# Tile 3's norm ahead of tile 4's statistics on VectorE, and its epsilon added there

## The chip, the cores and the metric

The kernel runs on one core of one Trainium2 chip. The metric is device time of one execution in microseconds (us), and the numbers quoted are medians of executions.

## The reference

```python
xn = _layernorm(x)                 # x: 2048 tokens x 1024, bf16
s  = attention(xn, wqkv, wo)       # 32 heads of 32
g  = silu(mlp(layernorm(xn)))      # 1024 -> 3584 -> 1024
return x + s * g
```

Only the first layer norm matters here. It is done by tiles of 128 tokens, 16 in all, in the first 35 us.

## The kernel before

All instructions are recorded first, in one order for each engine, with semaphores from the data dependences. These parts touch the change (cuts are marked):

```python
def bn_half(tb, c):   # statistics of half a tile, VectorE
    op("vector", lambda e: e.bn_stats(stats[:, tb, c, :], ...), ...)      # L324
def bn_merge(tb):
    op("vector", lambda e: e.bn_aggr(mv[:, tb, :], ...), ...)             # L328
def stat(tb):
    bn_half(tb, 0); bn_half(tb, 1); bn_merge(tb)

def rstd(lo, hi):     # 1/sqrt(var + eps)
    op("vector" if hi == 1 else "gpsimd", ... e.tensor_scalar(L(0), mv[:, lo:hi, 1], EPS, ...))   # L338
    op("gpsimd", ... e.tensor_tensor(L(2), L(0), mhalf[...], op=ALU.pow))                          # L340

def xnorm(tb):        # (x - mean) * rstd, 128x1024 bf16, VectorE
    op("vector", ... e.tensor_scalar(xnb[i], xst[...], mv[:, tb, 0:1], lnp[:, 2, tb:tb + 1], ...)) # L359

def transp(tb):       # tiles 0 to 5: TensorE (L386), copied out by ScalarE
    if tb >= TDMA:    # TDMA = 6: the others by a DMA transpose (L379)
        op("sync", lambda e: e.dma_start_transpose(xnT[:, :, tb * 128:(tb + 1) * 128], xnb[i]), ...)
    ...

def norm_pair(p):
    lo, hi = 2 * p, 2 * p + 2
    if p == 0:
        stat(0); rstd(0, 1); stat_scalar(1); xnorm(0); xnorm(1)
        stat(2); rstd(2, 3); stat(3); xnorm(2); rstd(3, 4)
    elif p == 1:
        stat(4); xnorm(3); stat(5); rstd(4, 6)
    else:
        if p < NP - 1: stat(hi)
        for t in (lo, lo + 1):
            xnorm(t)
            if t >= TDMA: transp(t)
        if p + 1 < NP: stat(hi + 1); rstd(hi, hi + 2)
    ...
```

(Several calls are put on one line here.) Each pair of tiles then gets its K and Q projections (L687), the transposes of a later pair (L386), its V projection (L703) and one step of attention (L867, L879, L896, L899).

The softmax here doesn't subtract the row's maximum and nothing guards it: scores larger than these inputs give would overflow.

Of the kernel before, what the change touches and what calls it, by code (L numbers as in the profile page):

```python
# [7 lines left out]
ALU = mybir.AluOpType  # L8
# [27 lines left out]
class _Prog:  # L36
# [52 lines left out]
    def op(self, eng, fn, r=(), w=(), dma=None, after=(), c=200.0):  # L89
        deps = list(after)  # L90
        rdy = self.ready(eng, r, w, after)
        same_raw = eng in ("vector", "scalar", "gpsimd")
        for k in r:
            o = self.lastw.get(k)
            if o is not None and (dma or o.dsem or o.eng != eng or same_raw):
                deps.append(o)
        for k in w:
            o = self.lastw.get(k)
            if o is not None and (dma or o.dsem or o.eng != eng or same_raw):
                deps.append(o)  # L100
            for o in self.readers[k].values():
                if dma or o.dsem or o.eng != eng or same_raw:
                    deps.append(o)
        dcount = None
        if dma:
            prev = self.dlast.get(dma)
            if prev is not None:
                deps.append(prev)
            dcount = 16 + (prev.dcount if prev is not None else 0)
        x = _Op(eng, len(self.lists[eng]), fn, deps, dma, dcount)  # L110
        if dma and self.dlast.get(dma) is not None:
            rdy = max(rdy, self.dlast[dma].t)
        self.clock(x, eng, dma, c, rdy)
        if dma:
            self.dlast[dma] = x
        self.lists[eng].append(x)
        self.order.append(x)
        for k in r:
            self.n += 1
            self.readers[k][(eng, self.n) if dma else eng] = x  # L120
        for k in w:
            self.lastw[k] = x
            self.readers[k] = {}
        return x
# [44 lines left out]
def bass_recurrent_scan__mha_block__mixer_channel_mlp__prompt_kernel(  # L169
# [28 lines left out]
    EPS = 1e-5  # L198
# [9 lines left out]
    with ExitStack() as st:  # L208
        pg = _Prog(nc, st)
        op = pg.op  # L210

        def sb(name, shape, dt):
            return st.enter_context(nc.sbuf_tensor(name, list(shape), dt))
# [30 lines left out]
        mv = sb("mv", [128, NT, 2], F32)  # L244
# [78 lines left out]
        def bn_half(tb, c):  # L323
            op("vector", lambda e: e.bn_stats(stats[:, tb, c, :], xst[:, tb * D + c * 512:tb * D + (c + 1) * 512]),  # L324
               r=[("xst", tb)], w=[("st", tb, c)], c=677.0)

        def bn_merge(tb):
            op("vector", lambda e: e.bn_aggr(mv[:, tb, :], stats[:, tb, :, :].rearrange("p c s -> p (c s)")),  # L328
               r=[("st", tb, 0), ("st", tb, 1)], w=[("mv", tb)], c=209.0)

        def stat(tb):
            bn_half(tb, 0)
            bn_half(tb, 1)
            bn_merge(tb)

        def rstd(lo, hi):
            L = lambda k: lnp[:, k, lo:hi]
            op("vector" if hi == 1 else "gpsimd", lambda e: e.tensor_scalar(L(0), mv[:, lo:hi, 1], EPS, None, op0=ALU.add),  # L338
               r=[("mv", t) for t in range(lo, hi)], w=[("l0", t) for t in range(lo, hi)], c=169.0)
            op("gpsimd", lambda e: e.tensor_tensor(L(2), L(0), mhalf[:, 0:hi - lo], op=ALU.pow), r=[("l0", t) for t in range(lo, hi)] + ["mhalf"],  # L340
               w=[("l2", t) for t in range(lo, hi)], c=708.0)

        def ycoef(b):
            lo, hi = 2 * b, 2 * b + 2
            L = lambda k: lnp[:, k, lo:hi]
            l2k = [("l2", t) for t in range(lo, hi)]
            mvk = [("mv", t) for t in range(lo, hi)] + [("var", 1)] * (b == 0)
            op("gpsimd", lambda e: e.tensor_tensor(L(4), mv[:, lo:hi, 1], L(2), op=ALU.mult), r=mvk + l2k, w=[("l4", b)])
            op("gpsimd", lambda e: e.tensor_tensor(L(4), L(4), L(2), op=ALU.mult), r=[("l4", b)] + l2k, w=[("l4", b)])
            op("gpsimd", lambda e: e.tensor_scalar(L(4), L(4), EPS, None, op0=ALU.add), r=[("l4", b)], w=[("l4", b)])  # L350
            op("gpsimd", lambda e: e.tensor_tensor(L(5), L(4), mhalf[:, 0:2], op=ALU.pow), r=[("l4", b), "mhalf"], w=[("l5", b)], c=760.0)
            op("gpsimd", lambda e: e.tensor_tensor(L(6), L(2), L(5), op=ALU.mult), r=[("l5", b)] + l2k, w=[("l6", b)])
            if b < 2:
                op("gpsimd", lambda e: e.tensor_tensor(L(7), mv[:, lo:hi, 0], L(6), op=ALU.mult), r=[("l6", b)] + mvk, w=[("l7", b)])
                op("gpsimd", lambda e: e.tensor_scalar(L(7), L(7), -1.0, None, op0=ALU.mult), r=[("l7", b)], w=[("l7", b)])

        def xnorm(tb):
            i = tb % NXN
            op("vector", lambda e: e.tensor_scalar(xnb[i], xst[:, tb * D:(tb + 1) * D], mv[:, tb, 0:1], lnp[:, 2, tb:tb + 1],  # L359
                                                   op0=ALU.subtract, op1=ALU.mult), r=[("xst", tb), ("mv", tb), ("l2", tb)], w=[("xnb", i)], c=545.0)  # L360
# [15 lines left out]
        def transp(tb):  # L376
            i = tb % NXN
            if tb >= TDMA:
                op("sync", lambda e: e.dma_start_transpose(xnT[:, :, tb * 128:(tb + 1) * 128], xnb[i]),  # L379
                   r=[("xnb", i)], w=[("xnT", tb)], dma=f"xt{tb % 4}", c=380)  # L380
                return
            bk = pro_bank()

            def f(e):
                for dc in range(DC):
                    ins = e.transpose(bankb(bk)[:, dc * 128:(dc + 1) * 128], xnb[i][:, dc * 128:(dc + 1) * 128], ident[:])  # L386
                return ins
            op("tensor", f, r=[("xnb", i), "ident"], w=[("b", bk)], c=("full", 8, 128))
            op("scalar", lambda e: e.activation(xnT[:, :, tb * 128:(tb + 1) * 128],
                                                bankb(bk)[:, 0:D].rearrange("p (c t) -> p c t", c=DC), ACT.Copy),  # L390
               r=[("b", bk)], w=[("xnT", tb)], c=903.0)
# [318 lines left out]
        def stat_scalar(tb):  # L710
            xt = xst[:, tb * D:(tb + 1) * D]
            mean, neg, sq = mv[:, tb, 0:1], mneg[:, 0:1], mneg[:, 1:2]
            op("scalar", lambda e: e.activation(xnb[8], xt, ACT.Identity, scale=-1.0 / D, accum_out=neg), r=[("xst", tb)], w=[("xnb", 8), "mneg"], c=903.0)
            op("scalar", lambda e: e.activation(xnb[8], xt, ACT.Square, bias=neg, accum_out=sq), r=[("xst", tb), "mneg"], w=[("xnb", 8), "msq"], c=903.0)  # L714
            op("scalar", lambda e: e.activation(mean, neg, ACT.Copy, scale=-1.0), r=["mneg"], w=[("mv", tb)], c=50.0)
            op("gpsimd", lambda e: e.tensor_scalar(lnp[:, 0, tb:tb + 1], sq, 1.0 / D, EPS, op0=ALU.mult, op1=ALU.add), r=["msq"], w=[("l0", tb)])
            op("gpsimd", lambda e: e.tensor_tensor(lnp[:, 2, tb:tb + 1], lnp[:, 0, tb:tb + 1], mhalf[:, 0:1], op=ALU.pow), r=[("l0", tb), "mhalf"],
               w=[("l2", tb)], c=708.0)
            op("gpsimd", lambda e: e.tensor_scalar(mv[:, tb, 1:2], sq, 1.0 / D, None, op0=ALU.mult), r=["msq"], w=[("var", tb)])
# [4 lines that stand above are left out]
                stat(0)  # L724
                rstd(0, 1)
                stat_scalar(1)
                xnorm(0)
                xnorm(1)
                stat(2)
                rstd(2, 3)  # L730
                stat(3)
                xnorm(2)
                rstd(3, 4)
            elif p == 1:
                stat(4)
                xnorm(3)
                stat(5)
                rstd(4, 6)
            else:
                if p < NP - 1:  # L740
                    stat(hi)
                for t in (lo, lo + 1):
                    xnorm(t)
                    if t >= TDMA:
                        transp(t)
                if p + 1 < NP:
                    stat(hi + 1)
                    rstd(hi, hi + 2)
            if p < 2:
                ycoef(p)  # L750
# [8 lines left out]
        for p in range(3):  # L759
            norm_pair(p)  # L760
# [186 lines left out]
        while u < NU + LAG or state["qi"] < total or dq or act_tasks or due:  # L947
# [13 lines left out]
            if u >= NP - 1 and state["qi"] < total:  # L961
# [8 lines left out]
                if entry:  # L970
                    it, lo, hi = entry
# [82 lines left out]
```

## Time and profile before

| | before |
|---|---|
| median of 3 runs at the outset | 1090.87 us (1089.76 to 1091.55) |
| span of the profiled run | 1087.7 us |
| TensorE, ScalarE, VectorE, GpSimd busy | 99%, 96%, 58%, 2% |
| transpose of tile 3 begins on TensorE | 13.29 us |
| chain on TensorE and ScalarE alone | from 13.3 us to nearly the end |

The prediction shows the views. One more line is needed, of the timeline of TensorE's weight loads (start, length, engine, line, what, idle time before it and what ended it; no bracket means no idle time):

```profile
13.29 0.45 PEld L386 LDWEIGHTS ps<-ident,hT 128*128 128x128 bf16 x8 [1.16 <-DVE hT L359]
...
17.58 0.99 PEld L386 LDWEIGHTS ps<-ident,hT 128*128 128x128 bf16 x16
```

Tile 3's transpose comes after 1.16 us of idle time, ended by VectorE's norm. The transposes of tiles 4 and 5 follow at 17.58 without a wait.

### The profile page before, as it was taken

To read this page: it belongs to the slowest core of one execution; us is meant where nothing else is said; L and a number is where in the kernel's file an instruction comes from. 1 tells how busy PE (TensorE), PEld (TensorE's weight loads), DVE (VectorE), ACT (ScalarE), POOL (GpSimd) and SP (SyncE) were. 2 spreads that over 40 slices of the span, in tenths; PEclk is the share of its full clock that TensorE was granted. 3 is DMA by queue.
4 is the path that set the end of the run, shared out by engine and by line. 5 is a ranking of instruction groups with operands and counts; after the bars stand their busy time and mean duration, and the time that the engine had idled before them with its cause. 6 is when DMAs were issued, how large, how long until landed. Compare 5 with 4: busy or idle time off the path is not lost.

```text
span 1087.7 us, 61820 instructions
## 1 busy us (share of the span) xinstructions
PE 1077.0 (99%) x29156; PEld 700.9 (64%) x29156; DVE 627.3 (58%) x1395; ACT 1043.5 (96%) x1197; POOL 22.6 (2%) x70
## 2 busy tenths in 40 slices
PE   8999999999999999999999999999999999999998
PEld 5766666666666666666666666666666666666665
DVE  7388843477732576642377743378733377635556
ACT  7899998999999999999999999999999999999993
POOL 4400000000000000000000000000000000000000
PEclk9999999999999999999999999999999999999999
DMA  8844365423364224345333264423254333675434
GB/s 247 169 139 137 111 172 149 121 61 110 109 164 122 65 63 120 109 104 148 90 100 100 69 161 119 125 81 109 81 132 119 91 119 108 198 201 107 108 92 124
DMA packets 209336, 131.92 MB, mean 121 GB/s; under 512 B 52538, under 2 KB 200250, under 8 KB 209082
## 3 DMA queue, kind: packets, MB, share of 16 engines
q1 hardware_dynamic: 209082, 127.97, 42.8%
q8 instruction: 228, 3.74, 1.4%
q14 instruction: 26, 0.21, 0.1%
HBM read 104.87 MB, written 12.06 MB: 107 GB/s over the span
## 4 chain that ended last, share of the span: by engine, by line
PE 54%; ACT 44%; DVE 1%; DMA 0%; issue 0%; POOL 0%; SPq 0%
ACT P L879 40%; PE ps L395 32%; PE ps L867 9%; PE ps L896 5%; PE ps L899 5%; ACT u L565 4%; PE ps L703 1%; PE ps L687 1%; ACT thz L609 0%; DVE stats L324 0%; DMA OT<-in_A_x_dram 0%; DVE wq L669 0%; PE ps L386 0%; DVE hT L359 0%; ACT hT L714 0%
## 5 line engine op out<-in xcount | busy, mean ns | idle before, releaser
L879 ACT ACTIVATE P<-ps 128x1024 bf16<-128x1024 f32 x1024 | 968.7, 1085 | 8.6 <-PE ps L867 4.0
L896 PE MATMUL ps<-P,VP 128*32 128x256 bf16 x4096 | 256.3, 273 | 0.0
L899 PE MATMUL ps<-P,ones 128*32 128x256 bf16 x4096 | 256.2, 273 | 0.0
L395 PE MATMUL ps<-yTc,war 128*32 128x352 bf16 (+1 forms) x5376 | 225.3, 309 | 0.0
L395 PE MATMUL ps<-hT,war 128*32 128x352 bf16 (+1 forms) x5376 | 225.2, 309 | 0.0
L867 PE MATMUL ps<-QT,KT 32*128 32x256 bf16 x4096 | 203.4, 273 | 2.9 <-ACT P L879 0.2
L395 PEld LDWEIGHTS ps<-hT,war 128*32 128x32 bf16 x5376 | 127.9, 96 | 73.9 <-issue 25.1
L395 PEld LDWEIGHTS ps<-yTc,war 128*32 128x32 bf16 x5376 | 127.4, 96 | 74.2 <-DVE xb L548 19.0
L867 PEld LDWEIGHTS ps<-QT,KT 32*128 32x128 bf16 x4096 | 60.7, 92 | 114.9 <-issue 60.0
L605 DVE TENSOR_SCALAR zh<-ps,b2h 128x352 f32<-128x352 f32 (+1 forms) x48 | 27.5, 572 | 182.3 <-PE ps L395 182.3
L571 DVE SCALAR_TENSOR_TENSOR hT<-u,xb 128x352 bf16<-128x352 f32 (+1 forms) x168 | 84.4, 510 | 68.4 <-ACT u L565 68.4
L548 DVE TENSOR_SCALAR xb<-ps,b1T 128x352 f32<-128x352 f32 (+1 forms) x168 | 96.3, 573 | 47.7 <-PE ps L395 42.8
L896 PEld LDWEIGHTS ps<-P,VP 128*32 128x32 bf16 x4096 | 109.1, 97 | 20.4 <-issue 1.3
L899 PEld LDWEIGHTS ps<-P,ones 128*32 128x32 bf16 x4096 | 109.2, 97 | 18.7
L395 PE MATMUL ps<-xnT,wq 128*32 128x352 bf16 (+1 forms) x2688 | 112.7, 309 | 0.0
L395 PEld LDWEIGHTS ps<-xnT,wq 128*32 128x32 bf16 x2688 | 63.7, 96 | 37.2 <-DVE xb L548 9.1
L558 DVE SCALAR_TENSOR_TENSOR u<-u,xb 128x352 f32<-128x352 f32 (+1 forms) x168 | 82.6, 510 | 1.9
L554 DVE TENSOR_TENSOR u<-xb 128x352 f32<-128x352 f32 (+1 forms) x168 | 82.6, 508 | 0.7
L565 ACT ACTIVATE u<-u 128x704 f32<-128x704 f32 (+1 forms) x84 | 71.9, 861 | 0.0
L395 PE MATMUL ps<-xnT,OT 128*32 128x352 bf16 (+2 forms) x1568 | 62.9, 306 | 0.2 <-DVE wq L669 0.2
L395 PE MATMUL ps<-wq,xnT 128*32 128x256 bf16 x1536 | 50.8, 274 | 0.0
L395 PEld LDWEIGHTS ps<-xnT,OT 128*32 128x32 bf16 x1568 | 37.7, 96 | 19.9 <-DVE wq L669 7.7
(61 smaller groups left out, 477.6 us busy)
## 6 DMA issues: line engine op xcount, KB each, us to landing
war<-in_B_w_dram SPq DMA_DIRECT2D x336, 256.0 KB, 3.3
wq<-in_A_wqkv_dram SPq DMA_DIRECT2D x36, 128.0 KB, 2.4
OT<-in_A_x_dram SPq DMA_DIRECT2D x16, 256.0 KB, 5.5
xnT<-in_A_x_dram SPq DMA_DIRECT2D x16, 256.0 KB, 3.2
out_dram<-wq SPq DMA_DIRECT2D x15, 256.0 KB, 2.0
y_scratch<-OT SPq DMA_DIRECT2D x14, 256.0 KB, 2.6
gT_scratch<-gst SPq DMA_DIRECT2D x32, 88.0 KB, 3.1
xnT<-in_A_wo_dram SPq DMA_DIRECT2D x8, 256.0 KB, 3.9
```

The costliest lines, as they stand in the source:

```text
L395: ins = e.matmul(outs(j), lhsT=lhs(j), rhs=rhs, start=start, stop=stop, tile_position=(0, 32 * j), skip_group_check=True)
L548: x0 = op("vector", lambda e: e.tensor_scalar(xb[:, 0:n], bank(bk, 0, n), b1T[:, f:f + 1], None, op0=ALU.add), r=[("b", bk), "b1"], w=[kx] ...
L554: x = op("vector", lambda e: e.tensor_tensor(ub[:, 0:n], xb[:, 0:n], xb[:, 0:n], op=ALU.mult), r=[kx], w=[ku], c=151 + 1.042 * n)
L558: x = op("vector", lambda e: e.scalar_tensor_tensor(ub[:, 0:n], ub[:, 0:n], 1.0 / 0.044715, xb[:, 0:n], op0=ALU.add, op1=ALU.mult), r=[kx, ...
L565: x = op("scalar", lambda e: e.activation(ut[:, :, 0:n], ut[:, :, 0:n], ACT.Tanh, scale=0.7978845608028654 * 0.044715), r=kus, w=kus, c=48 ...
L571: op("vector", lambda e: e.scalar_tensor_tensor(hT[:, fq, 0:n], ut[:, i, 0:n], 1.0, xq[:, 0:n], op0=ALU.add, op1=ALU.mult), r=[kus[i], kq] ...
L605: x0 = op("vector", lambda e: e.tensor_scalar(zh[:, 0:n], bank(bk, 0, n), 0.25, b2h[:, nb:nb + 1], op0=ALU.mult, op1=ALU.add), r=[("b", bk ...
L687: ins = e.matmul(bank(bk, off, off + 256), lhsT=wq[:, which, dc, 0:128], rhs=xnT[:, dc, t0:t0 + 256], start=dc == 0, stop=dc == DC - 1, sk ...
L867: ins = e.matmul(bank(bks[j], kh * 256, (kh + 1) * 256), lhsT=KT[i2][32 * j:32 * j + 32, k0:k0 + 128], rhs=QT[i2][32 * j:32 * j + 32, qb * ...
L879: op("scalar", lambda e, p=p, sl=sl: e.activation(pb[:, 2 * p:2 * p + 2, :, :].rearrange("p a b q -> p (a b q)"), ps[:, sl * 1024:(sl + 1) ...
L896: e.matmul(bankq(ACC, j, 0, QW), lhsT=VP[vp][:, kb, vo + 32 * j:vo + 32 * j + 32], rhs=pb[:, j, kh, :], start=first, stop=False, tile_posi ...
L899: ins = e.matmul(bankq(ACC, j, QW, 2 * QW), lhsT=ones[:, 0:32], rhs=pb[:, j, kh, :], start=False, stop=last, tile_position=(0, 32 * j), sk ...
```

## The change

TensorE waits for tile 3's norm while VectorE works on the statistics of tile 4. The change turns these two round. So that the norm finds its factor sooner, epsilon is added on VectorE, right after the merge, and GpSimd is left with the power alone.

```diff
-            op("vector" if hi == 1 else "gpsimd", lambda e: e.tensor_scalar(L(0), mv[:, lo:hi, 1], EPS, None, op0=ALU.add),
+            op("vector" if hi in (1, 4) else "gpsimd", lambda e: e.tensor_scalar(L(0), mv[:, lo:hi, 1], EPS, None, op0=ALU.add),
...
                 stat(3)
+                rstd(3, 4)
                 xnorm(2)
-                rstd(3, 4)
+                xnorm(3)
             elif p == 1:
                 stat(4)
-                xnorm(3)
                 stat(5)
                 rstd(4, 6)
```

## The prediction

> **What bounds the kernel now.** I read the page first, then the chain of waits, then the timeline of the first 35 us, which is all that the change touches.
>
> ```profile
> PE 1077.0 (99%) x29156; PEld 700.9 (64%) x29156; DVE 627.3 (58%) x1395; ACT 1043.5 (96%) x1197; POOL 22.6 (2%) x70
> PE 54%; ACT 44%; DVE 1%; DMA 0%; issue 0%; POOL 0%; SPq 0%
> ```
>
> The first line is busy time by engine, the second the share of each engine in the chain that ended last. TensorE and ScalarE bound the kernel in turn; VectorE has 1% of the chain, about 11 of 1087.7 us, and that piece lies in the opening. The chain over the first 16 us shows it:
>
> ```profile
> 7.60 0.55 DVE hT L359
> 8.15 1.21 DVE stats L324 x2
> 9.38 0.21 DVE mv L328
> 9.59 1.16 DVE stats L324 x2
> 10.77 0.21 DVE mv L328
> 10.98 0.41 DVE hT L359
> 11.39 1.21 DVE stats L324 x2
> 12.62 0.21 DVE mv L328
> 12.83 0.42 DVE hT L359
> 13.30 0.62 PE ps L386 x8
> 13.92 1.75 PE ps L703 x16
> ```
>
> Columns: start, length, what. From 7.60 VectorE works without a break: statistics of tiles 2 and 3, norm of tile 2 (10.98), statistics of tile 4 (11.39 to 12.83), norm of tile 3 (12.83 to 13.25). Then TensorE transposes tile 3 (L386) and is in the chain alone until 56.3 us, where ScalarE takes over. So tile 4's statistics, 1.44 us, stand in the chain ahead of the one norm that TensorE waits for. That is what the change attacks. TensorE idles there for 1.16 us by its own row, further down.
>
> GpSimd's timeline tells why the norm was put behind the statistics:
>
> ```profile
> 11.06 0.41 POOL L338 TENSOR_SCALAR lnp<-mv 128x1 f32<-128x1 f32 x1 [0.52 <-DVE mv L328]
> 11.55 0.56 POOL L340 TENSOR_TENSOR lnp<-lnp,mhalf 128x1 f32<-128x1 f32 x1
> 12.95 0.86 POOL L351 TENSOR_TENSOR lnp<-lnp,mhalf 128x2 f32<-128x2 f32 x1
> ```
>
> Tile 3's epsilon add takes 0.41 (0.22 for tile 2 at 9.67) and its power ends at 12.11, well after tile 2's norm is issued; the statistics fill that hole.
>
> **What the Trainium skill says.** (1) "SBUF — State Buffer", section "Who interferes with whom": VectorE's two-port modes, which a tensor_scalar can enter, take a port pair that GpSimd needs, for the whole instruction, and the one that comes second waits. The trace agrees for an operation that starts inside a norm: the add at 11.06 ends at 11.47, 0.08 after the norm of tile 2 ended (11.39); the power at 12.95 ends at 13.81, 0.57 after the norm of tile 3 ended (13.24), and it takes 0.86 against 0.70 for the same one, undisturbed, at 35.49. A norm that starts just after a GpSimd operation is not visibly delayed (34.33: 0.55). (2) "Perfetto Trace Analysis", section "DMA Instruction — HWDGE (DVE, Sync)": the profiled span of a DMA instruction leaves out the data movement. The trace agrees: the transposes' issues take 1.3 us at the median, and their landings 2.7 to 5.4, so landings have to be looked at by themselves. No other page bears on the argument.
>
> **The change, part by part.** *Added on VectorE:* one 128x1 add. Tile 0's twin started 0.24 after its merge (4.98 to 5.22) and took 0.15. Tile 3's merge starts at 10.77, so the add runs 11.01 to 11.16. VectorE starts a next instruction about 0.09 before the one ahead ends, so tile 2's norm moves from 10.89 to about 11.08, ending 11.58 in place of 11.39. That costs nothing at first: TensorE takes it up at 11.59 already.
>
> *Moved from GpSimd:* the add of 0.41 goes. The power would start 0.09 after the VectorE add, at 11.25, as at tile 0 (5.37 to 5.46). Alone it would end at 11.81. But tile 2's norm began at 11.08, so by point (1) it is held until 11.58. The two-column power ended 0.57 after release and 0.14 of its free 0.70 lay before it, so the one-column one, 0.56 free, should end 0.42 after release: 12.00. The intended gain loses 0.2 here.
>
> *Moved on VectorE:* tile 3's norm starts at about 12.04 in place of 12.75 and, from an idle engine, takes 0.55 (as at 7.60): it ends at 12.59 against 13.24. TensorE starts 0.05 later: 12.65 for 13.30. **Gain at this point 0.65 us.** The V weights, which TensorE needs next, were issued at 6.25 and landed 6.4 later, at 12.65; their matmuls would begin at 13.05, so they are there just in time.
>
> *What it costs:* VectorE now idles from 11.49 (tile 2's norm let go) to 12.04, 0.55, and has the add, 0.19, and 0.05 of a slower restart. Tile 5's statistics start at 13.94 in place of 13.15: **everything after it on VectorE is late by 0.79 us**, and it stays so, since VectorE is busy without a hole up to 33 us (next idle: 1.13 before 34.33).
>
> *Who meets that delay.* Tiles 4 and 5: their norms end at 17.26 and 17.74, where they ended at 16.47 and 16.95. TensorE started their transposes at 17.58; at 0.65 earlier it would want them at 16.93. It gets them at 17.31 and 17.79, so is done at about 18.25 with the weight loads; the V matmuls behind them started at 18.73, held by ScalarE's copy of Q, which itself moves 0.65 earlier (to about 18.08). So 18.25 against 18.73: **the gain shrinks to about 0.48.** Tiles 6 to 15 are transposed by DMA, at issues which follow VectorE's norms within 0.05 us. Tiles 6 and 7 landed at 23.0 and 24.5 for a use at 25.95: 1.5 us of room, enough. Tiles 8 and 9 are the tight ones:
>
> ```profile
> 30.43 0.66 PEld L687 LDWEIGHTS ps<-xnT,wq 128*128 128x128 bf16 x7 [0.21 <-DMA xnT<-hT]
> ```
>
> This is TensorE's weight-load timeline: the only matmuls of the opening that the profile puts down to a DMA transpose. The DMA view of the window around tile 9's issue (25.19) gives its landing, and that of tile 10's for comparison follows:
>
> ```profile
> xnT<-hT SPq DMA_TRANSPOSE x1, 5.1
> ...
> xnT<-hT SPq DMA_TRANSPOSE x1, 3.5
> ```
>
> 25.19 plus 5.1 is 30.3, and TensorE starts at 30.43 with an idle time (0.21) no longer than at its other changes of mode. So tile 9 lands with 0.1 us to spare. It lands late since the DMA engines stop in the middle of it: by the stretches they moved 143 GB/s from 26 to 27 us, then 20 and 5, then 207 from 29 to 30. A delay of 0.79 at the issue can therefore come straight out on TensorE. From 34 us on tiles have about 2 us of room.
>
> **The rivals.** *A, the gain lives.* The pause of the transfers does not recur, or falls elsewhere; tile 9 lands about 28.8 (2.8 after an issue at 26.0, as tiles 6 to 8 did). Then 0.48 us is kept to the end, for the whole later program is a chain of TensorE and ScalarE: 1090.87 - 0.48 = 1090.4. *B, a wait on DMA takes the place of the wait on VectorE.* The landing moves with its issue, 30.3 to 31.1: TensorE starts at about 31.1 for 30.43, and the kernel is slower by 0.7 in spite of the gain: 1091.6. For it: the idle time already attributed to this DMA. *C, the pause keeps its place in time* (27 to 29 us). Half of tile 9's data moved before it; now nearly all moves after it. The second half took 1.0 us (29.3 to 30.3), so the whole lands about 0.5 later: slower by about 0.45, 1091.3. *D, reordering.* The program places its later instructions by an internal clock estimate, so other choices could follow hundreds of us later. Once TensorE leads, all engines' clocks move together, and VectorE idles 14 us before 49.35, which resets its lag; I expect few or no changed places, but this is the main risk in the tails.
>
> **Range and chances.** I weigh A 0.35, B 0.35 and C 0.30: 0.35 x (-0.48) + 0.35 x 0.7 + 0.30 x 0.45 = +0.2, so 1091.0 from 1090.87 with rounding. The three runs of before spread over 1.8 us, more than the distance between the rivals, so the range is rival A less 1.0 and B plus 0.9: 1089.4 to 1092.5. Two per cent is 21.8 us, and the whole span ahead of the transpose at 13.30 holds no such amount: same 0.985, faster 0.005, slower 0.01.
>
> **What would show each step right or wrong.** In the changed profile: a VectorE add at about 11.0; GpSimd's power for tile 3 longer than 0.56, about 0.75, ending near 12.0 (at 11.8 the lock was wrong); TensorE's transpose of tile 3 at 12.65; statistics of tile 6 at 15.4 for 14.59; the transposes of tiles 4 and 5 now waiting on the norm, and the V matmuls behind them at about 18.25; tile 8's DMA transpose issued at 24.7 for 23.92; then the matmuls of 30.43 either at 29.95 (A) or at 30.9 to 31.1 with an idle time above 0.5 put down to the DMA (B, C). The prediction is wrong if the order of instructions after 50 us differs, if V's weights land after 13.05, or if the time leaves the range in fast runs.

## The result

The changed kernel took 1091.01 us (median of 6, 1089.12 to 1092.92), the kernel before 1090.66 us in the same rounds (median of 6, 1089.76 to 1091.55). The ratio is 1.0002 with a 95% interval of 0.9988 to 1.0017: the same. (A ratio is the mean time of one kernel's runs over that of the other's of the same rounds, so not quite the ratio of the medians.) On every engine the instructions stand in the same order as before, except for the moved ones.

The page of the changed kernel, busy time and chain by engine:

```profile
PE 1077.4 (99%) x29156; PEld 700.9 (64%) x29156; DVE 627.6 (58%) x1396; ACT 1043.4 (96%) x1197; POOL 22.5 (2%) x69
...
PE 55%; ACT 43%; DVE 1%; DMA 0%; POOL 0%; issue 0%; SPq 0%
```

One instruction went from GpSimd to VectorE; all else stayed. The chain of waits of the first 60 us (start, length, what) shows what happened:

```profile
9.66 1.16 DVE stats L324 x2
10.84 0.22 DVE mv L328
11.09 0.17 DVE lnp L338
11.32 0.80 POOL lnp L340
12.14 0.55 DVE hT L359
12.69 1.21 DVE stats L324 x2
13.92 0.21 DVE mv L328
14.12 1.16 DVE stats L324 x2
15.31 0.21 DVE mv L328
15.52 1.16 DVE stats L324 x2
16.71 0.21 DVE mv L328
16.92 0.44 DVE hT L359
17.40 1.07 PE ps L386 x16
```

Tile 3's norm now starts at 12.14 in place of 12.75, after a power on GpSimd that takes 0.8 us. The chain no longer passes to TensorE at tile 3. It stays on VectorE for three more tiles of statistics and reaches TensorE at 17.40, with the transposes of tiles 4 and 5. The weight loads that answer to those shown of before, and the K and Q projections that follow tile 9:

```profile
12.74 0.45 PEld L386 LDWEIGHTS ps<-ident,hT 128*128 128x128 bf16 x8 [0.53 <-DVE hT L359]
...
17.39 0.90 PEld L386 LDWEIGHTS ps<-ident,hT 128*128 128x128 bf16 x16 [0.38 <-DVE hT L359]
...
29.99 1.64 PEld L687 LDWEIGHTS ps<-xnT,wq 128*128 128x128 bf16 x16 [0.21 <-DMA xnT<-hT]
```

The idle time of 1.16 us became 0.53 us at tile 3 and 0.38 us, which is new, at tile 4. At 29.99 there is no added wait for the DMA transpose: 0.21 us is what TensorE idles at its other changes of mode (from one kind of matmul to the next) too. So 0.44 us was won by 30 us (29.99 for 30.43).

**Does it reach the end?** ScalarE runs 1024 exponentials (L879), the same in both kernels. Laying one trace's start times against the other's gives a shift for each. In the changed kernel it is -0.44 us at the third exponential (20.75 for 21.19), at the ninth, at the 901st it is -0.43, and -0.44 at the last; the span is 0.4 us shorter. In these two traces the rest of the program moved as one piece. The times do not show it, since they spread by 4 us.

### The profile page after: what moved, and what is told of

It is laid out like the page before. It is cut to its first block, busy times and chain, and to the rows that moved or that the text cites. A ratio compares the mean times of both kernels' runs of the same rounds, so it can differ in the third digit from the quotient of the medians.

```text
span 1087.2 us, 61820 instructions
## 1 busy us (share of the span) xinstructions
PE 1077.4 (99%) x29156; PEld 700.9 (64%) x29156; DVE 627.6 (58%) x1396; ACT 1043.4 (96%) x1197; POOL 22.5 (2%) x69
## 4 chain that ended last, share of the span: by engine, by line
PE 55%; ACT 43%; DVE 1%; DMA 0%; POOL 0%; issue 0%; SPq 0%
ACT P L879 39%; PE ps L395 33%; PE ps L867 9%; PE ps L896 6%; PE ps L899 6%; ACT u L565 4%; PE ps L703 1%; PE ps L687 1%; DVE stats L324 1%; ACT thz L609 0%; DMA OT<-in_A_x_dram 0%; DVE wq L669 0%; DVE hT L359 0%; ACT hT L714 0%; DVE zh L605 0%
## 5 line engine op out<-in xcount | busy, mean ns | idle before, releaser
L879 ACT ACTIVATE P<-ps 128x1024 bf16<-128x1024 f32 x1024 | 968.4, 1083 | 8.6 <-PE ps L867 3.9
```

Of the source, the lines that this page charges most:

```text
L879: op("scalar", lambda e, p=p, sl=sl: e.activation(pb[:, 2 * p:2 * p + 2, :, :].rearrange("p a b q -> p (a b q)"), ps[:, sl * 1024:(sl + 1) ...
```

## The experiments

Shifts below are against the first trace of before, **counted from the start of tile 2's statistics** in each trace (8.06 us in before), which takes out differences of up to 0.3 us in when the first loads land. So counted, the change stands at -0.51. The expectations count in two other ways. Those of after_again, order_only, add_only, fill, lag1, lag2, before_again and order_again take the shift as it stands ("uncounted" below), which is -0.44 for the change. Those of shift, shift_lag1 and fill_again count from tile 1's norm, which gives the same as here unless tile 2's load lands late. "Taken up" is when TensorE loads weights for the projections that need tile 9.

| run | third exp. | ninth exp. | 901st | last | tile 9 issued, landed | taken up (idle before) | median us (n) |
|---|---|---|---|---|---|---|---|
| before | 0 | 0 | 0 | 0 | 25.19, 30.29 | 30.43 (0.21) | 1090.66 (6) |
| before_again | 0.00 | 0.00 | +0.09 | +0.75 | 25.15, 30.24 | 30.38 (0.21) | one run |
| change | -0.51 | -0.51 | -0.51 | -0.51 | 26.05, 29.79 | 29.99 (0.21) | 1091.01 (6) |
| after_again | -0.52 | -0.53 | -0.53 | -0.53 | 26.02, 29.82 | 29.96 (0.21) | 1090.89 (5) |
| order_only | -0.35 | +0.47 | +0.47 | +0.58 | 26.03, 30.76 | 30.80 (1.03) | 1091.05 (5) |
| order_again | -0.35 | +0.04 | +0.67 | +3.79 | 26.24, 30.53 | 30.57 (0.60) | one run |
| add_only | +0.07 | +0.07 | +0.23 | +0.34 | 25.31, 30.25 | 30.55 (0.21) | 1090.28 (5) |
| fill | -0.57 | -0.57 | -0.22 | +0.16 | 25.34, 29.17 | 29.78 (0.21) | 1090.09 (5) |
| fill_again | -0.56 | -0.56 | +0.20 | +0.21 | 25.61, 29.37 | 30.05 (0.21) | 1090.73 (5) |
| lag1 | -0.52 | -0.20 | -0.20 | +0.28 | 26.66, 30.15 | 30.19 (0.53) | one run |
| lag2 | -0.52 | -0.24 | -0.07 | +1.50 | 27.24, 30.05 | 30.09 (0.49) | one run |
| shift | -0.52 | -0.52 | +0.02 | +2.06 | 26.75, 29.55 | 30.01 (0.21) | one run |
| shift_lag1 | -0.51 | -0.51 | +0.34 | +0.89 | 26.99, 29.80 | 30.19 (0.21) | one run |

The third exponential falls at about 21 us, ahead of all use of DMA transposes; the ninth at 34.6 us, behind tile 9. All runs were correct; four repeat another kernel, so that accidents of one execution show.

### after_again: the change once more

No edit.

> The changed kernel, unaltered, a second time. Theory (VectorE chain): the gain in the opening is about 0.45 us, it is set by 20 us and then carried unchanged to the end, so in the trace each exponential (ScalarE, the 1024 activations of P) starts about 0.4 to 0.5 us earlier than its twin in the kernel before. Rival (DMA decides): the landing of tiles 8 and 9, which came within 0.2 us of its use in both traces so far, is late in some executions; then this profile shows a wait over 0.3 us on a DMA transpose before the fifth K and Q projection of the opening, and the shift of the exponentials behind it differs from -0.44 by more than 0.2. Time: both theories say within 0.2% of before.

Measured: ratio 1.0000 (0.9987 to 1.0012), and -0.53 from end to end, or -0.46 uncounted. Tile 9 was in time again. This agrees with the first theory and goes against the DMA deciding in this execution.

### order_only and order_again: the order without the moved add

```diff
-            op("vector" if hi in (1, 4) else "gpsimd", ... EPS ...
+            op("vector" if hi == 1 else "gpsimd", ... EPS ...
```

> The order of the change alone, epsilon still added on GpSimd. Theory: GpSimd's add is held by tile 2's norm (0.41 us), its power ends at about 12.1, so tile 3's norm starts at 12.15, only 0.1 us later than in the change, and tile 6's statistics 0.9 us later than before (change: 0.8). Shift of the late exponentials against before: -0.35, against -0.44 of the change; the order carries four fifths of the gain. Rival (the move of the add carries it): tile 3's norm waits for GpSimd nearly as long as it did behind the statistics, shift about 0. Time: within 0.2%.

> The order alone, the same kernel a second time. In its first profile tile 9 landed at 30.8 in place of 29.8, although it was issued within 0.03 us of the change's. Theory (the length of the pause varies from execution to execution): shift of the late exponentials -0.44 if the pause ends before 28.5, and up to +0.4 if it doesn't; by the five profiles so far -0.44 is likelier. Rival (the edit makes the long pause): +0.38 again with a pause from 26.4 to 28.7.

Timeline of GpSimd in order_only, and its weight loads behind tile 9:

```profile
10.98 0.41 POOL L338 TENSOR_SCALAR lnp<-mv 128x1 f32<-128x1 f32 x1 [0.52 <-DVE mv L328]
11.47 0.56 POOL L340 TENSOR_TENSOR lnp<-lnp,mhalf 128x1 f32<-128x1 f32 x1
```

```profile
30.80 1.64 PEld L687 LDWEIGHTS ps<-xnT,wq 128*128 128x128 bf16 x16 [1.03 <-DMA xnT<-hT]
```

In the opening both runs give -0.35: the order carries two thirds of the -0.51, and the moved add 0.16 of it. The -0.35 expected was uncounted and four fifths of the change's -0.44; that the figures agree is chance, for uncounted the shift of order_only is -0.44. On GpSimd the add was held by tile 2's norm (0.41), whereas on VectorE it is the power that is held (0.78 for 0.56). So the move saves only part of what it removes.

Then tile 9 landed late. It was issued at the same time as in the change (26.03 for 26.05) and landed 1 us later, 30.76 for 29.79. TensorE waited 1.03 us, and the gain became a loss of 0.47. In the second run the same kernel waited 0.60 us and came out at +0.04. This is the prediction's rival B or C, which the change's own traces don't show. My expectation that the second run would likelier be at -0.44 was a miss (uncounted it came to +0.15). Whether the lateness belongs to this edit (two of two) or to chance stays open: its tile 9 is issued as in the change, but the two samples on each side are few.

### add_only: the add without the order

```diff
-            op("vector" if hi == 1 else "gpsimd", ... EPS ...
+            op("vector" if hi in (1, 4) else "gpsimd", ... EPS ...
```

(applied to the kernel before)

> The add on VectorE alone, the old order (statistics of tile 4 ahead of tile 3's norm). Theory: VectorE's queue, not GpSimd's power, holds tile 3's norm, so an earlier power is worth nothing, and the add puts about 0.1 us into the chain: tile 3's norm at 12.85 in place of 12.75, shift of the exponentials +0.1. Rival: the power was what held it; shift -0.1 or more. Time: within 0.2%.

Measured: +0.07 at the third and the ninth exponential. Tile 3's norm started at 12.87 (12.82 counted, 12.75 before): the added instruction costs its slot on VectorE. What an earlier power is worth this run does not test, since the power did not come earlier: here the add stands behind tile 2's norm (at 11.37), and the power runs from 11.59 to 12.14, from 11.55 to 12.11 before. That it would be worth nothing in the old order follows from before itself, where the power ends 0.64 us ahead of the norm.

### fill and fill_again: half of tile 4's statistics in the hole

```diff
-                xnorm(2)
-                xnorm(3)
+                xnorm(2); bn_half(4, 0)
+                xnorm(3)
             elif p == 1:
-                stat(4)
+                bn_half(4, 1); bn_merge(4)
```

> The change, and one half of tile 4's statistics (0.60 us on VectorE) put into the hole in which tile 3's norm waits for GpSimd's power. Theory: VectorE's hole of 0.55 us was what ate part of the gain at tiles 4 and 5; filled, tile 3's norm starts at about 12.2, at most 0.1 us later than in the change, and tiles 4 to 15 are only about 0.25 us later than before in place of 0.8; TensorE no longer waits for the norms of tiles 4 and 5, so the shift of the exponentials is -0.55 to -0.6 if tile 9's DMA transpose lands in time. Rival (ScalarE's copies or the DMA bound this stretch, not VectorE): -0.44 as in the change or less. Time: within 0.2%.

> The version that was ahead of both in the opening, a second time. Theory: counted from the norm of tile 1, its exponentials 2 and 8 are at -0.56 again to 0.03; tile 9 lands with over 0.3 us of room. What follows after 100 us are holes in TensorE's stream at other places than in the first profile. Time against before: inside the spread, ratio between 0.998 and 1.001.

Weight loads in fill, tile 3 and then tiles 4 and 5:

```profile
12.65 0.45 PEld L386 LDWEIGHTS ps<-ident,hT 128*128 128x128 bf16 x8 [0.59 <-DVE hT L359]
...
16.93 0.99 PEld L386 LDWEIGHTS ps<-ident,hT 128*128 128x128 bf16 x16
18.09 0.99 PEld L703 LDWEIGHTS ps<-wq,xnT 128*128 128x128 bf16 x10 [0.17 <-ACT QT L693]
```

The wait of 0.38 us at tiles 4 and 5 is gone, which shows that VectorE's hole caused it, and the shift is -0.57 and -0.56. But that is only 0.05 us more than the change, where 0.11 to 0.16 had been expected: the V projections behind (L703) now wait for ScalarE's copy of Q (L693), as they did in before. So the rival, that ScalarE's copies bound this stretch, is right once the hole is filled. What filling the hole gives besides is room: tile 9 lands 0.6 us ahead of its use. In fill_again tile 2's load landed at 8.22 us (7.67 in before) and pushed the whole opening back by 0.24 us; counted from tile 1's norm, as its expectation was, the shift was -0.32, a miss that this late load explains. By the time alone fill is the same as before: ratios 0.9998 (0.9986 to 1.0011) and 0.9997 (0.9982 to 1.0011). It is ahead of both kernels in the opening, and its medians are 0.4 us below those of before in both calls, but nothing here proves it faster.

### lag1 and lag2: VectorE later still, ahead of tile 8

One or two halves of statistics (0.60 us each) computed again, between the norms of tiles 7 and 8; to the change:

```diff
-                    stat(hi + 1)
+                    [bn_half(hi + 1, c) for c in range(1 * (p == 3))]; stat(hi + 1)     # lag2: range(2 * ...)
```

> The change with one more half of statistics (0.60 us on VectorE, the same numbers once again into the same place) between the norms of tiles 7 and 8. Nothing that TensorE or ScalarE does is altered; the DMA transposes of tiles 8 to 15 are issued 0.6 us later. Theory (tile 9's landing stands within 0.2 us of being the limit): it lands at 30.2 to 30.7 where TensorE wants it at about 29.9, the wait is put down to the DMA transpose, and the shift of the exponentials against before goes from -0.44 to between -0.1 and +0.4. Rival (the landing has real room, VectorE's lag is harmless): -0.44.

> Two such halves, 1.2 us. Theory: tile 9 lands between 30.6 and 31.3, the wait grows by up to as much, shift of the exponentials between +0.3 and +1.0, and the step lies between the 6th and the 8th exponential as in the run of the order alone. Rival (room): -0.44. Rival (the landing is set by the pause of the transfers alone, not by the issue): the same shift as with one half.

Weight loads behind tile 9, lag1:

```profile
30.19 1.64 PEld L687 LDWEIGHTS ps<-xnT,wq 128*128 128x128 bf16 x16 [0.53 <-DMA xnT<-hT]
```

and lag2:

```profile
30.09 1.64 PEld L687 LDWEIGHTS ps<-xnT,wq 128*128 128x128 bf16 x16 [0.49 <-DMA xnT<-hT]
```

With 0.6 us more lag the DMA transpose does become the limit: the shift falls from -0.52 to -0.20 between the third and the ninth exponential, a little short of the expected -0.1 to +0.4. So the change has less than 0.6 us of room. But twice the lag costs no more (-0.24, where +0.3 to +1.0 was expected: a miss; the rival on record with the same shift as lag1 has the number). Tile 9's landing is not its issue plus a constant: 5.1 us after it in before, 3.7 in the change, 3.5 in lag1, 2.8 in lag2.

### shift and shift_lag1: TensorE's instruction blocks come earlier

What makes up the difference is a silence of the transfers between 26 and 29 us. In the traces it lies beside one 16 KB packet on the queue that the page calls "instruction". In before, the transfers are silent from 27.07 to 28.53 and that packet ends at 28.50; in order_only silent to 27.95, packet ends at 27.92 (it took 1.89 us, against 0.98 in the change); in add_only 28.40 and 28.37. The full rate returns later still: in before the transfers move 7 to 12 GB/s for another 0.8 us, and about 290 only from 29.3. In lag2 the packet (25.79 to 26.68) ended before tile 8's data began to move (26.9), and both tiles landed 2.8 us after their issues: that is why its longer lag cost no more. These packets come once every 256 or so TensorE instructions. So six of TensorE's warming matmuls (each 128x512) were cut into four pieces each, which puts 36 more instructions ahead of the packet:

```diff
-            for i in range(k):
-                ins = e.matmul(bank(0), lhsT=ident[:], rhs=cold, ...
+            for i in range(k if k == 13 else 4 * k):
+                ins = e.matmul(bank(0) if k == 13 else bank(0, 0, 128), lhsT=ident[:], rhs=cold if k == 13 else ident[:], ...
```

> The change, with six of TensorE's warming matmuls before 10 us (128x512) each cut into four of 128x128: the same work, 36 more TensorE instructions (weight load and matmul) in its stream, nothing else altered. In all ten profiles the transfers fall silent beside a 16 KB packet of the instruction queue, and these packets come once every 256 or so TensorE instructions (the second after about 475, at 26.5 us in the change). Theory (that fetch makes the pause): with 36 more instructions ahead of it, the packet comes about 1.4 us earlier, near 25.1, before tile 8's data move; tiles 8 and 9 then land about 2.8 us after their issues (tile 9: 26.05 + 2.8 = 28.9, against 29.8), and no silent stretch lies between 26.2 and 28.9. Shift of the exponentials, counted from the norm of tile 1, stays -0.5, since tile 9 was in time in the change too. If the packet hits tile 7's data, tile 7 is late for its use at 25.5 and the shift shrinks there. Rival (the pause belongs to the transposes or to a moment, not to the fetch): silence at 26.5 to 28.4 as before, tile 9 at 29.8.

> The same 36 instructions added to the kernel with one more half of statistics ahead of tile 8. There tile 9 was issued at 26.66, landed at 30.15, TensorE waited 0.5, and the shift counted from the norm of tile 1 fell from -0.52 to -0.20. Theory (the fetch, not the lag alone, makes tile 9 late): fetch near 25.0, tile 9 lands at 29.5, no wait over 0.21, shift -0.5 kept. Rival (issue and queue alone): 30.15 and -0.20 again.

Stretches of one us (busy time of each engine, granted clock, share of the DMA engines' time, GB/s last), first the change, then shift:

```profile
27.00:28.00 1.00, 1.00 (x11) 0.90 (x10) 0.97 (x4) 1.00 (x2) 0.71 (x1) 1.00 1.71 23
```

```profile
27.00:28.00 1.00, 1.00 (x12) 0.90 (x10) 0.96 (x4) 1.00 (x2) 0.71 (x1) 1.00 0.58 126
```

The packet came at 25.04 in place of 26.56, as planned, mostly into the hole between the data of tiles 7 and 8, where nothing moves in the change either (24.8 to 25.95). From 27 to 28 us the transfers moved 126 GB/s in place of 23. Tiles 8 and 9 landed 3.3 and 2.8 us after their issues (4.2 and 3.7 in the change). Tile 9 landed at 29.55, not at 28.9 as expected: the issue of tile 8 itself, which ran beside the packet, took 1.9 us in place of 1.24 and held up the next, and tile 8's data still slowed to 10 to 33 GB/s from 26.5 to 27.0, which was not expected. In shift_lag1 the packet came at 25.26 and ended at 26.46, before tile 8's data (26.9); tile 9 landed at 29.80 (expected 29.5) and TensorE did not wait:

```profile
30.19 1.64 PEld L687 LDWEIGHTS ps<-xnT,wq 128*128 128x128 bf16 x16 [0.21 <-issue]
```

The 0.32 us that lag1 lost between the third and the ninth exponential are not lost (-0.51 and -0.51). As in fill_again, tile 2's load was late here, by 0.33 us, which is why the shift from tile 1's norm was -0.18 and not -0.5. Moving the instruction packet took the silence from the data of tile 9; nothing else in the program was altered. So the fetch of instructions beside the transposes is what makes tile 9 late, in these two runs against their twins. Why a fetch stops the other transfers was not tried.

### before_again, and where the rest of the time goes

> The kernel before, unaltered, a second profile. If a pause of the transfers near 27 to 29 us is there in each execution, tile 9 lands at 30.2 to 30.6 and the exponentials lie within 0.2 us of the first profile's; holes in TensorE's instruction stream that no wait explains (0.1 to 0.4 us, seen after 490 us in three of the traces) come at other places. If before's tile 9 is late in this one, the shift is +0.3 or more from the 8th exponential on.

Up to the ninth exponential this run equals the first one to 0.00 us; at the end it is 0.75 us later. What differs are idle times of TensorE which no wait explains. They lie past 100 us and at other places in each execution. The largest are in order_again; its waits of weight loads from 948 to 970 us (in total, times, longest), and the same of before:

```profile
PEld ps L395 <- issue: 4.2, 9, 1.5
```

```profile
PEld ps L395 <- issue: 1.7, 8, 0.2
```

Idle times put down to "issue", that is to nothing the profile shows, reach 1.5 us there, against 0.2 at each usual change of mode. Added up inside runs of one kind of weight load, past 10 us, such holes (longer than 0.15 us) come to 0 in before and in both traces of the change, 1.2 us in before_again, 0.75 in fill, 1.5 in lag2, 2.6 in shift and 4.1 in order_again. From the ninth to the last exponential these kernels lose 0, 0.75, 0.73, 1.74, 2.58 and 3.75 us. The holes account for most of what these profiled executions differ by after the opening. The traces also tell what they are. There are 27 in nine traces, and all 27 stand at the same place in TensorE's count of weight loads and matmuls, 193 or 194 past a multiple of 256, in shift too, whose count is 36 ahead. Each ends 1.2 to 1.6 us after the end of a packet of the instruction queue; the packet ahead of the longest hole took 2.44 us, where the median in that trace is 0.99. So TensorE stood there for a block of instructions that came late. No run made a fetch late on purpose.

## Why the prediction was right, and where it was not

**The time.** 1091.01 us against 1091.0, inside the range, class same. The agreement to a hundredth is luck: 1091.0 was a mean of three rivals, two of which expected a loss (and the sum gives 1091.08), and the spread of the executions, 3.8 us, is over eight times the effect.

**The opening, right step by step.** Numbers as in the trace of the change, which began 0.07 us later. The add ran at 11.09 (said 11.01). The power was held by tile 2's norm: 0.78 us and end at 12.10 (said 0.75 and 12.0; without the lock 11.8). Tile 3's norm started at 12.14 (12.04), its transpose at 12.74 (12.65). Tile 6's statistics started at 15.44 (15.4), so the lag of VectorE is there. The transposes of tiles 4 and 5 waited for it, from 17.39 (17.31), and the V projections followed at 18.25 (18.25). The gain of 0.65 that shrinks to 0.48 was measured as 0.51 once the late start is taken out. order_only, add_only and fill, each expected from the same working, came within 0.1 us of it in the opening, counted or not.

**The rivals, weighted wrongly.** The step that failed is "A delay of 0.79 at the issue can therefore come straight out on TensorE", with 0.65 of the weight on B and C. In both traces of the change rival A held. The issue of tile 9 moved by 0.86 us and its landing came 0.5 us earlier. But A's own account, landing at 28.8 without a pause, was wrong as well: the pause came, only it hit tile 8, which landed 4.2 us after its issue. C had left the pause in its place, to 29.3. But the instruction packet came 1.0 us earlier than in before (26.56 for 27.56), and the full rate was back at about 28.3. TensorE's lead of 0.44 us explains part of that 1.0; what set the rest is not shown. Tile 9 then landed within 0.2 us of its use. That B and C were no fancy is shown by order_only, where the same issue time ended in a wait of 1.03 us and a net loss, and by lag1. Which of the two ways the change's other executions went can't be said: the profiled ones were the fastest of their sets.

**What was not foreseen.** The prediction named a reordering of instructions as the risk in the tails. The order did not change. Between the profiled executions the differences come from holes in TensorE's stream of up to 4 us in sum and from loads of tile 2 that land up to 0.6 us later, neither of which was among the rivals. The prediction took it that no page beyond its two bears on the argument; the section on instruction fetch that the list at the end names does. Most executions have no trace, so what spreads the times of all of them is not shown.

## What to carry to other kernels

When one engine's queue feeds another, putting the wanted instruction first moves the delay onto everything behind it; look for who meets that delay, and fill the hole that the reordering opens (here half a tile's statistics, which gave 0.05 us at once and 0.4 us more room for the transpose), rather than leave the engine idle. Ask of every transfer how long before its use it lands, not how long it takes, since one with 0.2 us to spare is decided by accidents. An effect of half a us in 1090 can be shown by aligning traces instruction by instruction, where times of single executions, which here spread by 4 us, can't show it. Look also for what all unexplained waits have in common: here one place in every 256 instructions.

## What the Trainium skill lacked or had wrong

- "Runtime: NRT & Kernel Launch", section "Instruction fetch mechanics", has the refill in blocks of 16 KiB or 256 instructions, which the traces agree with (one packet of 16,384 bytes every 256 or so TensorE instructions), and calls the cost of a block boundary mostly hidden, of which the next point has the exceptions. It doesn't say that a fetch can hold up other transfers: beside it the DMA transposes fell silent for up to 1.5 us (27.07 to 28.53 in before) and reached their full rate only 0.8 us later, and with the fetch moved 1.5 us earlier the rate between 27 and 28 us rose from 23 to 126 GB/s.
- The same section gives no size for what a late block costs TensorE. Holes that no wait explains, all at one place in a block of 256 instructions, reached 1.52 us at a time and 4.1 us in one execution; four of the thirteen traces have none above 0.15 us among weight loads of one kind.
- "DMA: Bandwidth & Descriptors", section "DMA Transpose (X-bar)", gives no time from issue to landing for one transpose of 128x1024 from SBUF to SBUF, and no spread; the one duration on another page is of a 128x128 tile. Here tile 9's transpose landed 2.8 to 5.1 us after its issue in thirteen traces.
